# Decay rows of a fused forgetting attention: full-height selection matmuls, row DMAs and dummy matmuls in place of 3-row matmuls

## The chip, the cores and the metric

The kernel runs on one core of one Trainium2 chip. A core has five engines with an in-order instruction stream each: TensorE (PE, with its weight loads shown apart as PEld), VectorE (DVE), ScalarE (ACT), GpSimd (POOL) and SyncE (SP), which here only issues DMAs. TensorE writes to PSUM, which ScalarE and VectorE read and GpSimd does not. The metric is the device time of one launch in microseconds, lower is better.

## The reference

Attention with a forget gate, followed by a gated feed-forward with a short convolution over the sequence. B = 8 batches, H = 8 heads, S = 576 positions, D = 64, model width 512, inner width 1024.

```python
scores = np.matmul(q, k.transpose(0, 1, 3, 2)) / np.sqrt(D)
cum    = np.cumsum(np.log(np.clip(f, 0.0001, 1.0)), axis=-1)
decay  = cum[:, :, :, None] - cum[:, :, None, :]      # cum at the query minus cum at the key
scores = np.where(causal, -1e9, scores + decay)        # causal: keys after the query
attn   = exp(scores - max) / sum                       # softmax over the keys
x      = (attn @ v), heads side by side                # (B, S, 512)
h      = np.maximum(x @ w_in, 0.0)                     # (B, S, 1024)
conv   = conv_w[0] * h[s-1] + conv_w[1] * h[s] + conv_w[2] * h[s+1]
out    = (h * sigmoid(conv)) @ w_out
```

## The kernel before

The work is cut into 16 half batches (hb 0 to 15, four heads each; batch b is half batches 2b and 2b+1) and, per batch, a feed-forward of eight blocks of 128 inner columns.

**Loads.** The queue of SP loads q and k of a half batch with transposing DMAs (line 168) into one of four tiles `qk0` to `qk3`, head dimension on the partitions. The fp32 input is taken as pairs of 16-bit words, so the 64 dimensions stand on the 64 odd partitions as bf16 and the even partitions hold the low halves, which are not wanted. For the first six half batches VectorE's `clamp` (line 175) sets the even partitions to zero; later ones get them overwritten by DMAs (`fill`).

**Decay.** The decay is added inside the score matmul: even partitions 0, 2 and 4 carry 1 and -1 on one side and cum, as a bf16 high and low part, on the other. `kc` (128 x 576, bf16) holds -8 cum of all 64 heads: high parts on partitions 0 to 63, low parts on 64 to 127. VectorE makes it at the start from f by a clip (line 292), a scan (295) and two steps (296, 297), with a logarithm on ScalarE in between. From `kc` the rows reach the matmuls in four ways:

- Half batch 0: `first_rows` copies rows of `kc` by small DMAs from POOL and ScalarE (lines 236 to 239) onto partitions 0, 2 and 4 of `qk0`, first for heads 0 and 1, then for 2 and 3.
- Half batches 1 to 3 (`0 < hb < NX`): the rows stay apart. `own_rows` copies them by POOL DMAs (line 184) onto three neighbouring partitions of a feed-forward tile, `hg0`, and each score matmul (line 328) is followed by one with only these three rows (line 332), added into the same PSUM block.
- Half batches 4 and 5: `rows_of` (lines 188, 189, POOL) copies them from a DRAM image of `kc` (`decay_image`) onto the even partitions after the clamp.
- From half batch 6 on: `fill` (lines 193, 195, SP) does this for all even partitions from constants and the image.

**Score blocks.** A head's lower triangle is cut into four diagonal blocks (128 x 128, `diag_scores`), four blocks of the rest (448, 64, 320 and 192 columns, `off_scores`) and a last 64-column block (`tail_scores`): nine matmuls and 1,600 columns per head. Two heads form a pair: one diag task (8 matmuls), two off tasks (4 each); a half batch has two pairs and one tail task (4). ScalarE takes the exponential (lines 355, 365, 340), POOL masks diag and tail (368, 343). One sweep of 40 matmuls (line 390) with ones gives the sums (`sums`), two with v give the product (`pv`); VectorE forms the reciprocal (398 to 400) and normalises into `xt` (407). v is loaded per batch (line 245) and cast (251, 253) by VectorE for batch 0 and by POOL after that.

**Feed-forward.** `ffn1` (8 matmuls, line 417), relu on ScalarE (421), convolution in two VectorE steps (427, 429), tanh on ScalarE (432), gate on VectorE (436), `ffn2` (lines 443, 448), evacuation and store. w_in and w_out are loaded and cast during the first half batches (lines 216, 222, 224; 227, 231).

**Order.** `ORDER` holds one string per engine with a letter for each task, written out for the whole program. `Plan.play` walks through the five strings with estimated durations to assign buffers, and emits the instructions in the strings' order; on the chip semaphores hold each task until its inputs are there. There are four PSUM tiles `ps0` to `ps3` for all TensorE tasks. Everything ahead of the strings (loads of half batches 0 and 1, constants, `kc`, clamps and rows of half batch 0) is emitted first, in code order.

The score matmuls, with the line numbers of the profile:

```python
325    def scores(ps, col, hb, h, k0, q0, n):
326        tq, tk = stq_t[hb % RING], stk_t[hb % RING]
327        apart = 0 < hb < NX
328        nc.tensor.matmul(ps[:, col:col + n], tk[:, h * S + k0:h * S + k0 + 128], tq[:, h * S + q0:h * S + q0 + n],
329                         start=True, stop=not apart)
330        if apart:
331            o = own[32 * (hb - 1):32 * (hb - 1) + 3]
332            nc.tensor.matmul(ps[:, col:col + n], o[:, h * S + k0:h * S + k0 + 128],
333                             o[:, HS + 64 + h * S + q0:HS + 64 + h * S + q0 + n], start=False, stop=True)
```

Of the kernel before, what the change touches and what calls it, by code (L numbers as in the profile page):

```python
# [84 lines left out]
def kernel(  # L85
# [11 lines left out]
    nc = tc.nc  # L97
# [15 lines left out]
    NX, NCL = 4, 6  # L113
# [18 lines left out]
    lit = cpool.tile([128, 5], FP32, name="lit")  # L132
    lii = cpool.tile([128, 2], I32, name="lii")
# [25 lines left out]
    own = hgx_t[0].bitcast(BF16)  # L159
# [11 lines left out]

    def clamp(hb, side, c0, c1):
        t = qk_t[hb % RING].bitcast(U16)[:, 0:2 * HS].rearrange("p (a x) -> p a x", a=2)
        t = t[:, :, c0:c1] if side is None else t[:, side, c0:c1]
        nc.vector.tensor_scalar(t, t, lim[:, 0:1], 0.0 if 0 < hb < NX else lim[:, 1:2], op0=ALU.mult, op1=ALU.add)
# [5 lines left out]
    def own_rows(hb):  # L181
        c, p = hb * HH, 32 * (hb - 1)
        for j, side, first in ((1, 1, c), (2, 1, BH + c), (0, 0, c)):
            nc.gpsimd.dma_start(own[p + j:p + j + 1, (0 if side else HS + 64):(HS if side else 2 * HS + 64)], kc[first:first + HH])
# [48 lines left out]
    def first_rows(p, eng, lows):  # L233
        c, t, o = slice(2 * p, 2 * p + 2), qk_t[0], 2 * p * S
        if lows:
            eng.dma_start(t[4:5, HS + o:HS + o + 2 * S], kc[BH + 2 * p:BH + 2 * p + 2])
        else:
            eng.dma_start(t[2:3, HS + o:HS + o + 2 * S], kc[c])
            eng.dma_start(t[0:1, o:o + 2 * S], kc[c])

# [24 lines left out]
    nc.gpsimd.iota(lii[:, 0:1], pattern=[[0, 1]], base=0, channel_multiplier=1)  # L265
    nc.gpsimd.dma_start(cwrow, moe_conv_w)
# [5 lines left out]
    nc.gpsimd.memset(own.bitcast(FP32)[0:96, HS // 2 + 32:HS + 32], ones2)  # L272
    nc.gpsimd.memset(own.bitcast(FP32)[0:96, 0:HS // 2 + 32], minus2)
# [5 lines left out]
    nc.vector.tensor_copy(lit[:, 0:2], lii)  # L279
    nc.vector.tensor_scalar(lit[:, 3:4], lit[:, 0:1], 2.0, None, op0=ALU.is_equal)  # L280
    nc.vector.tensor_scalar(lit[:, 4:5], lit[:, 0:1], 4.0, None, op0=ALU.is_equal)
    nc.vector.tensor_tensor(lit[:, 3:4], lit[:, 3:4], lit[:, 4:5], op=ALU.add)
    nc.vector.tensor_scalar(lim[:, 1:2], lit[:, 3:4], float(0x3F80), None, op0=ALU.mult)
# [3 lines left out]
    for t in range(NVA):  # L287
        nc.vector.memset(va_t[t][64:128, :, NKB - 1, :], 0.0)
# [394 lines left out]
```

## Time and profile before

| | |
|---|---|
| Median of 3 runs | 298.72 us (294.78 to 300.27) |
| The profiled run | 294.69 us, span of its profile 293.0 us |
| Busy: PE, DVE, ACT, POOL | 265.8, 222.2, 203.5, 89.4 us |
| Weight loads (PEld) | 169.1 us |
| TensorE clock granted, mean over the span | 0.911 |
| DMA | 49.34 MB, mean 168 GB/s |

The profile is one execution, taken by the hardware profiler. A busy TensorE need not be a fast one: the granted clock (PEclk, 1.00 is full) stands beside it. "Idle before, releaser" says what an engine waited for. A line number with L is that of the kernel before, unless the text says otherwise; "x8" counts instructions.

### The profile page before, as it was taken

How to read it: one execution, taken by the hardware profiler on the slowest of the kernel's cores; microseconds unless marked ns; L12 is line 12 of the kernel's file. 1: busy time of each engine (PE TensorE's matmuls, PEld its weight loads, DVE VectorE, ACT ScalarE, POOL GpSimd, SP SyncE). 2: the span in 40 equal slices, each digit the busy share in tenths (PEclk: the TensorE clock that was granted, in tenths of full speed). 3: DMA queues.
4: the chain of work that ended last, by engine and by line, in shares of the span. 5: the costliest groups of instructions: out<-in, count | busy, mean ns of one | idle time of the engine just before them, and what ended most of it. 6: DMA issues, size and time to landing. Idle time of an engine off the chain costs nothing.

```text
span 293.0 us, 8211 instructions
## 1 busy us (share of the span) xinstructions
PE 265.8 (91%) x3508; PEld 169.1 (58%) x3508; DVE 222.2 (76%) x320; ACT 203.5 (69%) x272; POOL 89.4 (31%) x117
## 2 busy tenths in 40 slices
PE   1089999999999999899999998999799989999992
PEld 1054466535546766666667576766566767566541
DVE  5620239622806999988989899999989989999881
ACT  4055441643655999798888898889789979757751
POOL 6636100313240437512240454215401834000000
PEclk9995558955955999999999999999999999999999
DMA  7999997980007999999999999999999950012124
GB/s 158 202 214 295 195 180 177 241 218 0 4 0 191 177 186 207 151 202 275 201 193 233 238 175 284 194 185 191 202 252 215 238 167 10 0 74 91 73 90 161
DMA packets 126201, 49.34 MB, mean 168 GB/s; under 512 B 113807, under 2 KB 119679, under 8 KB 126166
## 3 DMA queue, kind: packets, MB, share of 16 engines
q1 hardware_dynamic: 125278, 48.00, 79.1%
q0 software_dynamic: 800, 0.68, 1.1%
q8 instruction: 27, 0.44, 0.7%
q10 hardware_dynamic: 88, 0.15, 0.1%
q14 instruction: 8, 0.07, 0.1%
HBM read 14.33 MB, written 10.03 MB: 83 GB/s over the span
## 4 chain that ended last, share of the span: by engine, by line
PE 72%; DVE 13%; DMA 5%; ACT 4%; issue 4%; POOL 1%; SPq 0%; DVEq 0%; ACTq 0%
PE ps L417 19%; PE ps L328 18%; PE ps L443 13%; PE ps L390 10%; PE ps L332 8%; DVE u L427 3%; DVE u L429 2%; DMA qk<-cz 2%; DVE xt L407 2%; PE ps L448 2%; DMA qk<-kc 2%; DVE hg L436 1%; PE ps L457 1%; DMA rb<-in_f_dram 1%; DVE rb L400 1%
## 5 line engine op out<-in xcount | busy, mean ns | idle before, releaser
L328 PE MATMUL ps<-qk 128*128 128x128 bf16 (+3 forms) x576 | 78.9, 256 | 13.6 <-DMA qk<-kc 10.1
L355 ACT ACTIVATE pp<-ps 128x1024 f16<-128x1024 f32 x64 | 64.8, 1026 | 23.5 <-PE ps L332 19.6
L417 PE MATMUL ps<-xt,w_in_f 128*128 128x288 f16 x512 | 72.5, 293 | 1.4 <-DVE xt L407 1.3
L368 POOL TENSOR_SCALAR_AFFINE_SELECT pp<-pd 128x1024 f16<-128x1024 f32 x32 | 38.0, 1195 | 95.3 <-ACT pd L365 95.3
L328 PEld LDWEIGHTS <-qk 128*128 128x128 bf16 x576 | 41.7, 100 | 39.2 <-issue 11.8
L427 DVE SCALAR_TENSOR_TENSOR u<-ht,cwt 128x576 f32<-128x576 f16 x64 | 55.3, 875 | 8.5 <-ACT ht L421 8.5
L417 PEld LDWEIGHTS <-w_in_f 128*128 128x128 f16 x512 | 50.0, 100 | 19.1 <-issue 2.4
L421 ACT ACTIVATE ht<-ps 128x576 f16<-128x576 f32 x64 | 41.4, 660 | 25.7 <-PE ps L417 23.0
L429 DVE SCALAR_TENSOR_TENSOR u<-ht,cwt,u 128x576 f32<-128x576 f16 x64 | 57.5, 906 | 0.6
L436 DVE SCALAR_TENSOR_TENSOR hg<-hg,ht 128x576 f16<-128x576 f16 x64 | 49.3, 787 | 11.3 <-ACT hg L432 11.2
L432 ACT ACTIVATE hg<-u,cw 128x576 f16<-128x576 f32 x64 | 48.9, 780 | 7.0 <-DVE u L429 6.9
L443 PE MATMUL ps<-w_out_f,hg 128*128 128x512 f16 x224 | 52.4, 379 | 0.0
L365 ACT ACTIVATE pd<-ps 128x1024 f32<-128x1024 f32 x32 | 32.7, 1028 | 15.9 <-PE ps L328 12.2
L443 PEld LDWEIGHTS <-hg 128*128 128x128 f16 x224 | 21.3, 98 | 21.7
L332 PE MATMUL ps<-hg 3*128 3x128 bf16 (+3 forms) x108 | 31.6, 293 | 0.0
L390 PE MATMUL ps<-pp,va 128*32 128x128 f16 (+3 forms) x1152 | 29.9, 258 | 1.6 <-issue 1.6
L407 DVE TENSOR_TENSOR xt<-ps,rb 128x576 f16<-128x576 f32 x32 | 23.6, 751 | 8.2 <-PE ps L390 7.7
L398 DVE STREAM_TRANSPOSE st<-ps 128x576 f32<-128x576 f32 x16 | 12.4, 776 | 22.8 <-PE ps L390 22.6
L390 PEld LDWEIGHTS <-va 128*32 128x32 f16 x1280 | 24.3, 105 | 8.6 <-issue 5.3
L343 POOL TENSOR_SCALAR_AFFINE_SELECT pt<-p 128x256 f16<-128x256 f32 x16 | 9.2, 575 | 44.8 <-ACT p L340 44.8
L468 ACT COPY ob<-ps 128x1024 f32<-128x1024 f32 (+1 forms) x23 | 18.2, 792 | 3.5 <-PE ps L457 1.5
L332 PEld LDWEIGHTS <-hg 3*128 3x128 bf16 x108 | 10.2, 95 | 14.5 <-issue 8.1
(77 smaller groups left out, 164.3 us busy)
## 6 DMA issues: line engine op xcount, KB each, us to landing
vf<-in_v_dram SPq DMA_DIRECT2D x32, 256.0 KB, 4.9
out_dram<-ob SPq DMA_DIRECT2D x16, 512.0 KB, 3.5
qk<-cz SPq DMA_DIRECT2D x10, 540.0 KB, 6.0
ob<-in_moe_w_out_dram SPq DMA_DIRECT2D x4, 512.0 KB, 6.3
vf<-in_v_dram SPq DMA_DIRECT2D x8, 128.0 KB
vf<-in_moe_w_in_dram SPq DMA_DIRECT2D x2, 512.0 KB, 5.5
hg<-in_moe_w_in_dram SPq DMA_DIRECT2D x2, 512.0 KB
out_dram<-ob SPq DMA_DIRECT2D x16, 64.0 KB
```

The lines of the kernel that those rows point to most:

```text
L328: nc.tensor.matmul(ps[:, col:col + n], tk[:, h * S + k0:h * S + k0 + 128], tq[:, h * S + q0:h * S + q0 + n], start=True, stop=not apart)
L332: nc.tensor.matmul(ps[:, col:col + n], o[:, h * S + k0:h * S + k0 + 128], o[:, HS + 64 + h * S + q0:HS + 64 + h * S + q0 + n], start=False ...
L355: nc.scalar.activation(pp_t[slot[t_dg, "p"]][:, 1024 * s:1024 * (s + 1)], ps_t[slot[t_sc, "ps"]], AF.Exp, scale=SCALE)
L368: nc.gpsimd.affine_select(pp_t[slot[t_dg, "p"]][:, 2048:3072].rearrange("p (m j) -> p m j", j=128), pd_t[slot[t_ex, "pd"]].rearrange("p (m ...
L390: nc.tensor.matmul(ps[32 * h:32 * (h + 1), AB + q0:AB + q0 + n], left_of(h, m), p, start=x in (0, 3), stop=x in (2, 9), skip_group_check=True)
L417: nc.tensor.matmul(ps[:, MB + 288 * a:MB + 288 * (a + 1)], w_in_f16[:, cc, 128 * ff:128 * (ff + 1)], xt[:, cc, 288 * a:288 * (a + 1)], sta ...
L421: nc.scalar.activation(ht_t[slot[t_m1, "ht"]][:, 1:1 + S], ps_t[slot[t_m1, "ps"]][:, MB:MB + S], AF.Relu, scale=0.5)
L427: nc.vector.scalar_tensor_tensor(u, ht[:, 0:S], cwt[:, ff, 0:1], ht[:, 1:1 + S], op0=ALU.mult, op1=ALU.add)
L429: nc.vector.scalar_tensor_tensor(u, ht[:, 2:2 + S], cwt[:, ff, 1:2], u, op0=ALU.mult, op1=ALU.add)
L432: nc.scalar.activation(hg_t[slot[t_g0, "hg"]][:, ff, :], u_t[slot[t_u, "u"]], AF.Tanh, scale=cw[:, ff, 1:2])
L436: nc.vector.scalar_tensor_tensor(hv, hv, 1.0, ht_t[slot[t_m1, "ht"]][:, 1:1 + S], op0=ALU.add, op1=ALU.mult)
L443: nc.tensor.matmul(o, hg[:, ff, 128 * c:128 * (c + 1)], w_out_f16[:, ff, :], start=(ff == 0), stop=(ff == NFF - 1))
```

## The change

Half batches 0 and 1 are now treated alike, half batches 2 and 3 like 4 and 5, and no 3-row matmul is left.

- **First pairs (heads 0 and 1) of half batches 0 and 1** (`apart`): no rows are copied. After each score matmul two full-height matmuls add the decay straight from `kc`: one with `kc` as weights and a moving operand that is one column of `sel_k` (it picks the head's high and low part) read n times, and one with `sel_q` as weights (-1 in the head's row) and `kc` as moving operand.
- **Their second pairs (heads 2 and 3)**: `own_rows` copies three rows by POOL DMAs onto partitions 0, 2 and 4 of the `qk` tile, after the clamp of that part.
- **Half batches 2 and 3**: `rows_of`, from the DRAM image, after the clamp. The tile `hg0` no longer holds rows, and its two preset memsets go.
- **Dummy matmuls** (`WARM`): 16 of 512 columns at the start on a tile of ones, and 4, 6 and 6 ahead of the first diag task of half batches 1, 2 and 3; their results are overwritten.
- The clamp of the first pair of half batch 0 moves ahead of logarithm and scan; half batch 1 is clamped in four parts instead of two. All five order strings are new.

```diff
-    NX, NCL = 4, 6
+    NCL = 6
+    WARM = {0: 16, 2: 4, 4: 6, 6: 6}
...
+    def apart(hb, h):
+        return hb < 2 and h < 2
...
-    def own_rows(hb):
-        c, p = hb * HH, 32 * (hb - 1)
-        for j, side, first in ((1, 1, c), (2, 1, BH + c), (0, 0, c)):
-            nc.gpsimd.dma_start(own[p + j:p + j + 1, ...], kc[first:first + HH])
+    def own_rows(hb, side):
+        c, t = hb * HH + 2, qk_t[hb % RING]
+        if side:
+            nc.gpsimd.dma_start(t[2:3, HS + 2 * S:HS + 4 * S], kc[c:c + 2])
+            nc.gpsimd.dma_start(t[4:5, HS + 2 * S:HS + 4 * S], kc[BH + c:BH + c + 2])
+        else:
+            nc.gpsimd.dma_start(t[0:1, 2 * S:4 * S], kc[c:c + 2])
...
+    nc.vector.memset(xt_t[0][:, 0, :], 1.0)
+    nc.vector.tensor_scalar(sel_k, hfx, lit[:, 2:3], None, op0=ALU.is_equal)
+    nc.vector.tensor_scalar(sel_q, hfx.unsqueeze(3).broadcast_to((128, 2, 2, 128)), lit[:, 0:1], -1.0,
+                            op0=ALU.is_equal, op1=ALU.mult)
+    for x in range(WARM[0]):
+        nc.tensor.matmul(ps_t[0][:, 0:512], xt_t[0][:, 0, 0:128], xt_t[0][:, 0, 64:576], start=True, stop=True)
...
     nc.vector.tensor_scalar(fsb, fsb, 1e-4, 1.0, op0=ALU.max, op1=ALU.min)
+    clamp(0, None, 0, 2 * S)
     nc.scalar.activation(fsb, fsb, AF.Ln)
...
-    for p in range(2):
-        clamp(0, None, 2 * p * S, 2 * (p + 1) * S)
-        first_rows(p, nc.gpsimd, False)
-        first_rows(p, nc.scalar, True)
-    own_rows(1)
+    clamp(0, None, 2 * S, 4 * S)
+    own_rows(0, 1)
+    own_rows(0, 0)
...
-        apart = 0 < hb < NX
-        nc.tensor.matmul(ps[:, col:col + n], tk[:, h * S + k0:h * S + k0 + 128], tq[:, h * S + q0:h * S + q0 + n],
-                         start=True, stop=not apart)
-        if apart:
-            o = own[32 * (hb - 1):32 * (hb - 1) + 3]
-            nc.tensor.matmul(ps[:, col:col + n], o[:, h * S + k0:h * S + k0 + 128],
-                             o[:, HS + 64 + h * S + q0:HS + 64 + h * S + q0 + n], start=False, stop=True)
+        o = ps[:, col:col + n]
+        nc.tensor.matmul(o, tk[:, h * S + k0:h * S + k0 + 128], tq[:, h * S + q0:h * S + q0 + n],
+                         start=True, stop=not apart(hb, h))
+        if apart(hb, h):
+            nc.tensor.matmul(o[0:m], kc[:, k0:k0 + m], sel_k[:, hb, h:h + 1].broadcast_to((128, n)),
+                             start=False, stop=False)
+            nc.tensor.matmul(o, sel_q[:, hb, h, :], kc[:, q0:q0 + n], start=False, stop=True)
...
     def diag_scores(me, i):
+        for x in range(WARM.get(i, 0) if i else 0):
+            nc.tensor.matmul(ps_t[slot[me, "ps"]][:, 0:512], kc[:, 0:128], kc[:, 64:576], start=True, stop=True)
...
-        "PE": "wdodtodooodtosopopsppffdftfoodoodffftodoofsoppsdpotpodoffffggfodtfogsodgoppofddsfoppoohoftffgfdo"
+        "PE": "wdootdodooosdtopopsppffffdodfofotfofddooostoppdosdopoptffffoggtdfdofosgdogpofpstddfpopooohffffgtd"
```

In the PE strings d is a diag task, o off, t tail, s sums, p pv, f ffn1, g ffn2, w the transposes of the convolution weights. Both programs do half batches 0 and 1, then ffn1 of batch 0 around half batches 2 and 3.

Three places where the instructions of an engine change. First TensorE where it passes from half batch 0 (tile `qk_78`, in the changed program `qk_82`) to the first diag task of half batch 1 (`qk_79`, then `qk_83`). Before:

```order
L328 LDWEIGHTS qk_78
L328 MATMUL ps_122<-qk_78 128x192
L328 LDWEIGHTS qk_79
L328 MATMUL ps_124<-qk_79 128x128
L332 LDWEIGHTS hg_117
L332 MATMUL ps_124<-hg_117 128x128
```

and changed (line 368 is a dummy, 336 the score matmul, 339 and 341 the selections):

```order
L336 LDWEIGHTS qk_82
L336 MATMUL ps_129<-qk_82 128x192
L368 LDWEIGHTS kc
L368 MATMUL ps_128<-kc 128x512
...
L336 LDWEIGHTS qk_83
L336 MATMUL ps_128<-qk_83 128x128
L339 LDWEIGHTS kc
L339 MATMUL ps_128<-sel_k,kc 128x128
L341 LDWEIGHTS sel_q
L341 MATMUL ps_128<-kc,sel_q 128x128
```

The pair of one full and one 3-row matmul per block has become three full ones, behind four dummies.

Second VectorE at the start, from the clip of f (`rb`) to the first row copies. Before:

```order
L292 TENSOR_SCALAR rb_106<-rb_106 128x576
L295 SCALAR_TENSOR_TENSOR rb_107<-one_73,rb_106 128x576
L296 TENSOR_SCALAR kc<-rb_107 128x576
L297 SCALAR_TENSOR_TENSOR kc<-rb_107,kc 64x576
L175 TENSOR_SCALAR qk_78<-qk_78,lim 128x2x1152 x2
L175 TENSOR_SCALAR qk_79<-qk_79,lim 128x2304
```

and changed:

```order
L301 TENSOR_SCALAR rb_110<-rb_110 128x576
L182 TENSOR_SCALAR qk_82<-qk_82,lim 128x2x1152
L305 SCALAR_TENSOR_TENSOR rb_111<-one_73,rb_110 128x576
L306 TENSOR_SCALAR kc<-rb_111 128x576
L307 SCALAR_TENSOR_TENSOR kc<-rb_111,kc 64x576
L182 TENSOR_SCALAR qk_82<-qk_82,lim 128x2x1152
L182 TENSOR_SCALAR qk_83<-qk_83,lim 128x1152
```

The first pair's clamp has moved ahead of the scan, and with it the scan waits for the first q and k.

Third POOL, from its first row copies on. Before:

```order
L238 DMA qk_78<-kc 1x2x576
L239 DMA qk_78<-kc 1x2x576
L238 DMA qk_78<-kc 1x2x576
L239 DMA qk_78<-kc 1x2x576
L184 DMA hg_117<-kc 1x4x576 x3
L343 AFFINE_SELECT pt_95<-p_101 128x256
L368 AFFINE_SELECT pp_88<-pd_99 128x1024
L184 DMA hg_117<-kc 1x4x576 x6
L368 AFFINE_SELECT pp_89<-pd_100 128x1024
```

and changed, from the last masks of half batch 1 on (`qk_84` and `qk_85` belong to half batches 2 and 3, `qk_82` now to 4):

```order
L378 AFFINE_SELECT pp_95<-pd_104 128x1024
L351 AFFINE_SELECT pt_100<-p_106 128x256
L198 DMA qk_84<-image 1x16x144
L199 DMA qk_84<-image 2x2304
L198 DMA qk_85<-image 1x16x144
L199 DMA qk_85<-image 2x2304
L351 AFFINE_SELECT pt_101<-p_105 128x256
L378 AFFINE_SELECT pp_96<-pd_103 128x1024
L378 AFFINE_SELECT pp_97<-pd_104 128x1024
L198 DMA qk_82<-image 1x16x144
L199 DMA qk_82<-image 2x2304
```

The rows of half batches 2 and 3, copied ahead of time from `kc` before, now pass POOL between masks and wait there for their clamps.

93 lines of the change are left out of this document (46 added, 47 removed), and 8 rows, old and new, of the table KINDS.

## The prediction

> **What bounds the kernel now.** I read the page's head first, then a table of stretches cut where the granted clock changes, then one source line in short windows, then waits, chain and transfers.
>
> ```profile
> span 293.0 us, 8211 instructions
> ...
> PEclk9995558955955999999999999999999999999999
> ```
>
> The clock row, 40 slices of 7.3 us, reads 5 tenths in seven of the first thirteen: a TensorE that is busy there is slow. The stretches (length, then busy time and instruction count of PE, PEld, DVE, ACT, POOL; clock; DMA share; GB/s):
>
> ```profile
> 15.90:22.40 6.50, 6.50 (x49) 4.59 (x49) 1.69 (x3) 4.54 (x6) 3.01 (x5) 1.00 1.15 227
> 22.40:46.30 23.90, 23.90 (x301) 12.53 (x298) 6.88 (x13) 9.70 (x11) 5.56 (x8) 0.50 1.16 218
> 46.30:60.00 13.70, 12.99 (x94) 7.56 (x83) 11.40 (x15) 7.07 (x10) 3.82 (x5) 1.00 0.93 220
> 60.00:73.60 13.60, 13.60 (x55) 6.11 (x55) 2.55 (x4) 4.71 (x6) 2.71 (x3) 0.50 0.33 86
> 73.60:80.50 6.90, 6.90 (x44) 3.94 (x42) 5.76 (x8) 4.29 (x7) 1.93 (x5) 0.99 0.03 4
> 80.50:94.10 13.60, 13.60 (x167) 7.03 (x170) 3.98 (x7) 7.58 (x9) 3.31 (x4) 0.50 0.33 84
> 94.10:286.20 192.10, 186.06 (x2806) 125.82 (x2794) 179.65 (x239) 161.32 (x222) 59.49 (x65) 1.00 0.84 173
> ```
>
> Two kernels stand here. From 94.1 the clock is full and both TensorE (186.06 of 192.10) and VectorE (179.65) are packed; I leave that stretch as it is. Before it lie 15.9 us of start and a front of 78.2 us, 51.1 of them at half clock with TensorE never idle and VectorE nearly so (2.55 of 13.60). Next, the 3-row matmuls of line 332 alone, in windows that each end at or next to a decision (busy time, count, clock, DMA share, GB/s), and their group on the page:
>
> ```profile
> 42.90:46.30 3.40, 0.00 (x0) 0.50 0.87 143
> 49.70:53.10 3.40, 1.69 (x9) 1.00 0.54 122
> 56.60:60.00 3.40, 2.33 (x10) 1.00 1.21 233
> 70.20:73.60 3.40, 0.00 (x0) 0.50 0.00 0
> 77.00:80.40 3.40, 2.29 (x11) 1.00 0.04 7
> ...
> L332 PE MATMUL ps<-hg 3*128 3x128 bf16 (+3 forms) x108 | 31.6, 293 | 0.0
> ```
>
> The clock fell after 56.6 to 60.0 and 77.0 to 80.4, where these fill over two thirds of the time, held after 49.7 to 53.1, where they fill half, and rose after the two windows with none. The changes lie 23.9, 13.7, 13.6, 6.9 and 13.6 us apart: 7, 4, 4, 2 and 4 times 3.41, so it is decided once per 3.41 us. The 2806 matmuls after 94.1 hold none of line 332, and the clock never falls. I conclude that a matmul that loads 3 of 128 rows hardly counts as work to whatever sets the clock.
>
> [...]
>
> **The change, part by part.** *Start.* The first scores wait for row DMAs:
>
> ```profile
> 2.96 1.59 SPq L168 DMA_TRANSPOSE qk<-in_q_dram  x1
> ...
> 6.01 1.55 SPq L168 DMA_TRANSPOSE qk<-in_q_dram  x1
> 6.19 1.36 DVE L295 TENSOR_TENSOR_SCAN rb<-one,rb 128x576 f32<-128x576 f32 x1 [0.75 <-ACT rb L293]
> 7.58 0.46 DVE L296 TENSOR_SCALAR kc<-rb 128x576 bf16<-128x576 f32 x1
> 8.08 0.76 DVE L297 SCALAR_TENSOR_TENSOR kc<-rb,kc 64x576 bf16<-64x576 f32 x1
> ...
> 10.12 0.88 DVE L175 TENSOR_SCALAR qk<-qk,lim 128x2304 uint16<-128x2304 uint16 x1 [0.38 <-DMA qk<-in_q_dram]
> ...
> 15.90 3.58 PE L328 MATMUL ps<-qk 128*128 128x128 bf16 x29 [10.06 <-DMA qk<-kc]
> ```
>
> The second q load, issued at 6.01, landed at 10.1, 4.1 later; the first, issued at 2.96, then lands at 7.0. The clamp that now stands ahead of the scan waits for it: 7.0 to 7.9; scan to 9.3, the two kc steps to 10.5, 1.7 later than today. But the first pair then needs no row DMA: scores at 10.5 instead of 15.9, a gain of 5.4. The new constants on VectorE (a memset, four small operations) fall where it waits for f and then for this load.
>
> The 29 first matmuls are 4,480 columns in 3.5 us, 1,280 columns per us: half of what follows below, so the clock was half there, whatever the 1.00 of that row. The 16 dummies (8,192 columns) then take at most 6.4 us, from about 1.6 to 8.0, in TensorE's empty time. They cost nothing and cover at least one whole window, so the clock is full by 8. From 8.0 to 10.5 it may drop again: then 3.4 us of selection work run at half, at most 1.7 us lost, ahead of a wait that hides it.
>
> *Matmuls.* Full-clock prices, from the chain after 94 and from a timeline in the stretch to 60.0:
>
> ```profile
> 142.06 0.98 PE ps L417 x8
> 143.15 0.81 PE ps L390 x40
> ...
> 145.05 0.88 PE ps L328 x12
> ...
> 58.42 0.23 PE L328 MATMUL ps<-qk 128*128 128x128 bf16 x1
> 58.58 0.23 PE L332 MATMUL ps<-hg 3*128 3x128 bf16 x1
> ```
>
> Eight ffn1 matmuls of 288 columns in 0.98 us give 2,350 columns per us. Selections: 4 heads, 9 blocks, 2 each, 72 matmuls of 12,800 columns, 5.4 us. No row has a moving operand that is one column read again and again; between ffn1's rate and that of the 3-row alternation (a start every 0.16 us per 128 columns, 800 per us) it is 5.4 to 16; a gain is excluded, since it is added work. I take 5.4: ffn1 has full-height weights too. Dummies inside the loop: 16 of 512 columns, 3.5 us, less where they fall into a wait. Gone: 31.6 us of line 332.
>
> *Second pair of half batch 0.* Its rows are now three DMAs on POOL after the second clamp (10.5 to 11.4).
>
> ```profile
> 10.05 1.05 POOL L238 DMA_DIRECT2D qk<-kc  x1 [3.78 <-DVE qk L175]
> 11.09 0.52 POOL L239 DMA_DIRECT2D qk<-kc  x1
> ...
> qk<-kc POOLq DMA_DIRECT2D x4, 2.2 KB, 4.7
> ...
> 41.09 1.02 ACT L355 ACTIVATE pp<-ps 128x1024 f16<-128x1024 f32 x1 [3.02 <-PE ps L332]
> ```
>
> First issue 1.05, the next 0.52 each: the third at 13.0, landed 4.7 later, 17.7. TensorE and, behind the tail, ScalarE stand until then (the new ScalarE order takes the tail third). From 17.9 twelve exponentials remain for half batches 0 and 1: ten of 1.03 and two of 0.38, 11.1 us, to 29.0. Today the last ends at 42.1, and ffn1 of batch 0 starts at 46.4; now it starts at 33.
>
> *The rest of the front.* By 94.1 today's TensorE has done half batches 0 to 3 without the last two pv, and eight ffn1. At full clock 12 score matmuls (eight of a diag, four of an off) take 0.88, and a half batch has two of these, two more off (0.88) and a tail (0.12, an estimate by columns), and three sweeps of 0.81: 5.2. Four less 1.6, plus 8 x 0.98, make 27. Four sums say when the new kernel can stand there:
>
> ```profile
> 44.92 6.11 SPq L245 DMA_DIRECT2D vf<-in_v_dram  x5
> ...
> vf<-in_v_dram SPq DMA_DIRECT2D x32, 256.0 KB, 4.9
> ...
> L355 ACT ACTIVATE pp<-ps 128x1024 f16<-128x1024 f32 x64 | 64.8, 1026 | 23.5 <-PE ps L332 19.6
> ...
> L427 DVE SCALAR_TENSOR_TENSOR u<-ht,cwt 128x576 f32<-128x576 f16 x64 | 55.3, 875 | 8.5 <-ACT ht L421 8.5
> ...
> L421 ACT ACTIVATE ht<-ps 128x576 f16<-128x576 f32 x64 | 41.4, 660 | 25.7 <-PE ps L417 23.0
> ...
> L436 DVE SCALAR_TENSOR_TENSOR hg<-hg,ht 128x576 f16<-128x576 f16 x64 | 49.3, 787 | 11.3 <-ACT hg L432 11.2
> L432 ACT ACTIVATE hg<-u,cw 128x576 f16<-128x576 f32 x64 | 48.9, 780 | 7.0 <-DVE u L429 6.9
> ```
>
> TensorE: 10.5 + 27 + 5.4 + 3.5 = 46.4. Loads: v of batch 1 is issued until 51.0, and the last of its five parts (issued near 50) lands near 55; the DMA share of 1.16 from 22.4 says that the queue is full to there, and the same transfers stand ahead of it in the new order, so it gains nothing; two casts on POOL (1.5 each, an estimate by the 1,280 elements beside a mask's 1.2 for 1,024) follow, and the sweeps that need them: 58 to 60. ScalarE: 24 exponentials of 1.03 and four of 0.38, 26.2; eight relu and eight tanh, 11.5; two casts of an exponential's size, 2.1; from 13, with 3 of waiting: 56. VectorE, from 33: eight times 2 x 0.875 + 0.787, 20.3, and some 9 (an estimate: three clamps at twice the 0.88 above, two reciprocals of about 1.8, a cast): 62 at most, since today's has not done all of it by 94.1. I take **60**, 34 earlier: the loads' and VectorE's sum, which end last.
>
> *Rows of half batches 2 and 3* now go clamp, POOL, DRAM image and back, as those of 4 and 5 do today:
>
> ```profile
> qk<-image POOLq DMA_DIRECT2D x2, 9.0 KB, 3.5
> ```
>
> A clamp of at most twice 0.88, two issues of 0.5 and 3.5 make about 6: for half batch 2, whose clamp follows batch 0's last norm at 33, ready at 39. TensorE has four ffn1 and four or six dummies until 38, so it waits 0 to 2, inside the 60. Without that cover it would be 6 for each of the two.
>
> *Loads after it.* Today SP stands still, and with it the DMA shares of 0.33, 0.03 and 0.33 above:
>
> ```profile
> SPq L227 <- ACT w_out_f L231: 26.0, 1, 26.0
> ```
>
> The fourth w_out load needs a buffer that a ScalarE cast frees, ScalarE waits for slow scores, and q, k and v queue behind. Full DMA ends near 60.0 + 0.33 x 13.6 = 64.5, and the queue goes on 26 later, near 90. With ScalarE on time the wait goes, and what follows comes after that one load, from about 66: 24 earlier, against TensorE's 34. Of the missing 10, ffn2 of batch 1 (five of 1.7) can be done first, and the lead of the loads covers some; I charge 2, with 0 to 9 as bounds.
>
> **Sum.** 293.0 - 34 + 2 = 261 of span; the profiled run has 1.7 around its span (294.69): 262.7, say **263**. The median of the runs before, 298.72, stands 1.4% above that profile; the same here would be 266.
>
> **Rivals.**
> 1. *The half clock has another cause* and stays. Then 31.6 us of 3-row work go, or 22 if only the spacing counts (0.16 of each 0.23), selections and dummies cost 17.8 at half clock, the start gives 5.4: 276 to 285. For it: other work changes too where line 332 stands. Against: the five windows above and the 192 us without a fall. 0.08. [...]
> 2. *The loads keep the end.* ScalarE again reaches the w_out cast late and SP stands 20 us or more; the loads then hardly move, and of 34 only ffn2's 8.7 and a lead of some 7 remain: 279. For it: the 26.0 above. Against: the wait comes from ScalarE waiting for slow scores. 0.09.
> 3. *Slower: POOL's in-order queue.* The row DMAs of half batches 2 to 5 wait for VectorE's clamps and stand ahead of masks; both pd buffers fill, ScalarE stops, no relu reaches VectorE, the clamp comes later still. Run one after another, each half batch costs clamp and rows 6, exponentials 6.6 and sums to norm some 6 (three sweeps and VectorE's part), 18.6 for 5.2 of TensorE: 13.4 lost, four times: 317. It decides against the change once each of the four row waits exceeds 9. Against: ScalarE and VectorE are over half idle in today's front. 0.02.
>
> **How the numbers follow.** Forecast 0.76, 263, with 252 to 274 its own range (the front done at 51 to 64, loads 0 to 9). Better than 251: 0.03, TensorE's sum of 46 with little in its way. Another 0.02 lies near no change. I give 251 to 279, which reaches into the first two rivals. About 2%, 6 us, is what a measurement here can tell from no change; every case but the third and the rest lies below 292.7: faster 0.95, same 0.03, slower 0.02.
>
> **What would show it.** Clock row without fives after slice 2; no line of 3-row matmuls; first scores near 10.5 and a TensorE pause until 17.7; first ffn1 near 33; v of batch 1 landing near 55; no 26 us wait on SP; a stretch of some 192 us at the end as packed as today's. I am wrong if the clock falls while full-height selections run, if SP's wait stays, or if VectorE has gaps after 60.

## The result and the profile after

The changed kernel takes 269.28 us (median of 4 runs, 267.36 to 272.60) against 297.25 us for the kernel before on the same chip (294.78 to 300.27): a ratio of 0.906, with a 95% interval of 0.893 to 0.919. The forecast was 263, 6 below. The profiled run took 268.24 us with a span of 266.5, where the sum had 261.

From the page of the changed kernel: head, busy times, granted clock in 40 slices (6.7 us each), and the row of the queue that SP fills (packets, MB, share of 16 engines' span; it was 79.1% before).

```profile
span 266.5 us, 8203 instructions
...
PE 236.8 (89%) x3501; PEld 158.2 (59%) x3504; DVE 224.5 (84%) x327; ACT 202.5 (76%) x272; POOL 85.5 (32%) x113
...
PEclk9989999999999999999999898999999999999998
...
q1 hardware_dynamic: 125278, 48.00, 90.5%
```

The row of fives is gone: the mean clock rose from 0.911 to 0.978. TensorE is busy 29 us less (265.8 before), with nearly the same instructions; DVE, ACT and POOL are busy as long as before. The front is read from its windows (length, busy time and count of PE, PEld, DVE, ACT, POOL; clock; DMA share; GB/s) and from the first ffn1 matmuls (min/median/max ns, first and last start in 30 to 70 us):

```profile
12.30:15.70 3.40, 3.40 (x19) 1.94 (x17) 2.07 (x9) 0.44 (x1) 1.55 (x4) 0.50 1.17 229
15.70:32.80 17.10, 14.85 (x334) 11.04 (x337) 9.37 (x16) 12.58 (x15) 8.45 (x12) 1.00 1.16 242
32.80:66.90 34.10, 25.96 (x448) 18.94 (x442) 33.85 (x40) 28.81 (x38) 17.24 (x21) 1.00 1.18 230
...
L427 PE MATMUL ps<-xt,w_in_f x95: 282/286/296, 33.1 to 70.0; 128*128 128x288 f16 x95
```

From 15.7 to 66.9 the clock is full; in the kernel before, 51.1 of the 78.2 us from 15.9 to 94.1 were at half. PE has idle time here again (25.96 of 34.10) while VectorE has none (33.85): in this part of the front VectorE and the loads now set the pace. By the starts in the trace, the work that TensorE had done at 94.5 in the kernel before (half batches 0 to 3 without two pv, and eight ffn1) is done at 60.6, 33.9 earlier.

The rest is where the missing microseconds lie. Two stretches behind the front, first of the kernel before, then of the changed one:

```profile
94.00:172.00 78.00, 76.22 (x1169) 52.62 (x1158) 72.64 (x97) 70.14 (x96) 28.49 (x32) 1.00 1.07 205
172.00:198.00 26.00, 24.99 (x473) 17.62 (x475) 25.38 (x35) 22.27 (x32) 10.85 (x13) 1.00 1.06 214
```

```profile
60.00:138.00 78.00, 74.35 (x1141) 50.25 (x1141) 71.72 (x96) 68.81 (x93) 30.41 (x35) 1.00 1.14 214
138.00:172.00 34.00, 28.57 (x498) 19.67 (x496) 24.44 (x35) 24.07 (x33) 10.60 (x11) 0.90 1.08 201
```

The first 78 us hold about the same number of instructions in both, and so does the stretch behind it (473 and 498 matmuls, 35 and 35 on DVE), which takes 34 us where it took 26. To compare kernels with different orders I marked, in each trace, when TensorE has done 27, 100 and 125 us of full-clock work in its own order (decay matmuls and dummies not counted). The marks are estimates from full-clock prices per matmul; two traces of the changed kernel differ by 1 to 2 us in them (60.6 and 59.3 below), so smaller differences say nothing:

| Work of TensorE | before | changed |
|---|---|---|
| first 27 us, done at | 94.5 | 60.6 |
| 27 to 100 | 76.9 | 78.5 |
| 100 to 125 | 26.8 | 34.1 |
| 125 to the last matmul | 88.9 | 87.8 |

Inside the 34 us, four windows show two pauses and their aftermath, and the chain of waits names what the second one waits for (start, length, what):

```profile
142.00:145.40 3.40, 0.85 (x18) 0.88 (x19) 2.52 (x3) 0.64 (x3) 0.45 (x1) 1.00 1.20 160
145.40:148.80 3.40, 3.40 (x54) 2.13 (x52) 0.51 (x1) 2.82 (x3) 2.35 (x4) 0.51 0.90 180
155.70:159.10 3.40, 1.05 (x46) 0.85 (x46) 3.04 (x6) 1.37 (x3) 0.00 (x0) 1.00 1.05 123
159.10:162.50 3.40, 3.40 (x36) 2.27 (x37) 1.41 (x2) 1.86 (x3) 1.22 (x2) 0.50 1.16 241
```

```profile
by line: DMA qk<-cz 23.8%; DMA qk<-in_q_dram 21.2%; PE ps L427 18.9%; PE ps L336 12.2%; SPq L172 9.8%; PE ps L400 8.8%; SPq L489 4.0%; issue 1.4%; SPq L203 0.1%
...
141.48 2.83 SPq L172
...
145.65 6.14 DMA qk<-in_q_dram
...
151.85 6.91 DMA qk<-cz
...
158.96 1.13 PE ps L336 x12
```

The chain runs through SP's queue: a k load, which is issued over 2.83 us once TensorE is through with line 427 at 141.48, then two stores, then the q load of half batch 11 with 6.14 us until it lands and its fill with 6.91, and only then scores. The first pause is a fill as well, that of half batch 10. The profile names VectorE's line 439 for this wait, but the weight load of the scores also waits for the fill's two DMAs, issued at 136.98 and 137.98, and they are complete only at 144.33, 0.2 us before the scores start. The DMA share in the windows is 0.90 to 1.20: the queue is full, and late. Each pause costs twice, since the clock is half in the window after it (0.51 and 0.50 with PE busy all through). The two waits were 3.08 and 2.35 us long, and in the windows ahead of the half clock PE was busy for 0.85 and 1.05 us of 3.40.

### The profile page after: what moved, and what is told of

It reads as the page before. It is cut to its first block, busy times and chain, and to the rows that moved or that the text cites. A ratio compares the mean times of both kernels' runs of the same rounds, so it can differ in the third digit from the quotient of the medians.

```text
span 266.5 us, 8203 instructions
## 1 busy us (share of the span) xinstructions
PE 236.8 (89%) x3501; PEld 158.2 (59%) x3504; DVE 224.5 (84%) x327; ACT 202.5 (76%) x272; POOL 85.5 (32%) x113
## 4 chain that ended last, share of the span: by engine, by line
PE 56%; DMA 13%; DVE 12%; SPq 7%; ACT 5%; issue 5%; DVEq 0%; ACTq 0%
PE ps L453 16%; PE ps L427 15%; PE ps L336 10%; PE ps L400 8%; DMA qk<-in_q_dram 6%; DMA qk<-cz 5%; SPq L172 4%; PE ps L467 3%; DVE u L437 2%; ACT pp L363 2%; DVE u L439 2%; DVE qk L182 2%; ACT pd L375 2%; DMA qk<-image 2%; PE ps L458 1%
## 5 line engine op out<-in xcount | busy, mean ns | idle before, releaser
L336 PE MATMUL ps<-qk 128*128 128x128 bf16 (+3 forms) x576 | 62.5, 244 | 15.7 <-DVE u L439 5.5
L427 PE MATMUL ps<-xt,w_in_f 128*128 128x288 f16 x512 | 71.6, 290 | 0.7 <-DVE xt L417 0.4
L378 POOL TENSOR_SCALAR_AFFINE_SELECT pp<-pd 128x1024 f16<-128x1024 f32 x32 | 40.3, 1264 | 77.5 <-ACT pd L375 77.4
L336 PEld LDWEIGHTS <-qk 128*128 128x128 bf16 x576 | 38.1, 99 | 31.6 <-issue 12.9
L439 DVE SCALAR_TENSOR_TENSOR u<-ht,cwt,u 128x576 f32<-128x576 f16 x64 | 55.5, 879 | 0.6
L446 DVE SCALAR_TENSOR_TENSOR hg<-hg,ht 128x576 f16<-128x576 f16 x64 | 51.8, 818 | 3.4 <-ACT hg L442 3.2
L400 PE MATMUL ps<-pp,va 128*32 128x128 f16 (+3 forms) x1152 | 26.7, 239 | 2.3 <-issue 1.9
L400 PEld LDWEIGHTS <-va 128*32 128x32 f16 x1280 | 21.8, 97 | 10.4 <-issue 8.3
L253 POOL CAST va<-vf 128x1024 f16<-128x1024 f32 x14 | 16.6, 1188 | 17.7 <-DMA vf<-in_v_dram 17.6
L400 PE MATMUL ps<-pp,ones_h 128*32 128x128 f16 (+3 forms) x576 | 14.4, 245 | 1.3 <-DVE xt L417 0.7
```

What stands on the lines that cost most here:

```text
L336: nc.tensor.matmul(o, tk[:, h * S + k0:h * S + k0 + 128], tq[:, h * S + q0:h * S + q0 + n], start=True, stop=not apart(hb, h))
L378: nc.gpsimd.affine_select(pp_t[slot[t_dg, "p"]][:, 2048:3072].rearrange("p (m j) -> p m j", j=128), pd_t[slot[t_ex, "pd"]].rearrange("p (m ...
L400: nc.tensor.matmul(ps[32 * h:32 * (h + 1), AB + q0:AB + q0 + n], left_of(h, m), p, start=x in (0, 3), stop=x in (2, 9), skip_group_check=True)
L427: nc.tensor.matmul(ps[:, MB + 288 * a:MB + 288 * (a + 1)], w_in_f16[:, cc, 128 * ff:128 * (ff + 1)], xt[:, cc, 288 * a:288 * (a + 1)], sta ...
L439: nc.vector.scalar_tensor_tensor(u, ht[:, 2:2 + S], cwt[:, ff, 1:2], u, op0=ALU.mult, op1=ALU.add)
L446: nc.vector.scalar_tensor_tensor(hv, hv, 1.0, ht_t[slot[t_m1, "ht"]][:, 1:1 + S], op0=ALU.add, op1=ALU.mult)
```

## The experiments

The theory: the whole gain is TensorE's clock, which the alternation with 3-row matmuls pulled down. Rivals: the new orders, the row DMAs or the dummies bring part of it; the clock fell for another reason; or the alternation costs time of its own, whatever the clock. Then, for the missing 6 us: the loads, or an engine's order. "before" in the ratios is the kernel before on the same chip (medians 295.97 and 295.79).

| Run | us | ratio to before, 95% interval | first 27 us done at | from there to the last matmul |
|---|---|---|---|---|
| before (profile shown) | | | 94.5 | 192.6 |
| changed (profile shown) | 269.28 | 0.906 (0.893 to 0.919) | 60.6 | 200.4 |
| e1 full rows | 267.04 | 0.899 (0.891 to 0.908) | 63.2 | 194.1 |
| e2 32 rows | 295.26 | 0.997 (0.991 to 1.002) | 92.4 | 193.5 |
| e3 no rows (one run) | 261.12 | | 60.2 | 193.4 |
| e4 3-row selection | 281.11 | 0.950 (0.944 to 0.956) | 75.4 | 198.5 |
| e5 changed kernel again | 269.70 | 0.912 (0.903 to 0.921) | 59.3 | 202.1 |
| e6 no dummies | 269.90 | 0.910 (0.901 to 0.919) | 62.2 | 201.9 |
| e7 less v | 257.76 | 0.869 (0.859 to 0.878) | 59.0 | 190.6 |
| e8 rows by DMA | 274.64 | 0.928 (0.921 to 0.935) | 74.0 | 193.3 |
| e9 64 rows | 294.96 | 0.998 (0.993 to 1.002) | 102.4 | 190.6 |
| e10 96 rows | 267.32 | 0.902 (0.895 to 0.909) | 60.5 | 196.2 |
| e11 selections only | 271.02 | 0.914 (0.910 to 0.918) | 66.9 | 195.9 |
| e12 clamp for half batch 9 | 267.95 | 0.903 (0.897 to 0.909) | 61.8 | 197.7 |

The last two columns are of the profiled run; that of e9 took 300.52 us, 5.6 more than its median, so its front is late by about as much. e1 to e3 and e8 to e11 stand on the kernel before and keep its orders, e8 but for a few places; e4 to e7 and e12 stand on the changed one.

### One part alone: the height of the extra matmul (e1, e2, e9, e10)

All four are the kernel before in its own order, with the operands of line 332 changed and little else. In e1, e9 and e10 the extra matmul adds a negligible term (a factor of 2^-20), so the decay of half batches 1 to 3 is left out. In e1 it is one matmul of all 128 partitions (line 334 there):

```diff
+    nc.gpsimd.memset(tiny, 2.0 ** -20)
...
-            o = own[32 * (hb - 1):32 * (hb - 1) + 3]
-            nc.tensor.matmul(ps[:, col:col + n], o[:, h * S + k0:h * S + k0 + 128],
-                             o[:, HS + 64 + h * S + q0:HS + 64 + h * S + q0 + n], start=False, stop=True)
+            kk = min(k0, S - 128)
+            nc.tensor.matmul(ps[:, col:col + n], kc[:, kk:kk + 128], tiny[:, 0:n], start=False, stop=True)
```

> The kernel before, with each 3-row matmul replaced by one full-height matmul of as many columns (weights from kc, a constant of 2^-20 as moving operand), so the decay of half batches 1 to 3 is left out; order, loads, waits and row DMAs stay. Theory A (3-row matmuls count as no work and lower the clock): no half clock after 22, ffn1 of batch 0 near 36 instead of 46, the later stretch of 192 us unchanged: 268 to 277 us. Theory B (the half clock has another cause, and the gain of the change comes from its orders, its start and its loads): clock falls as before, 290 to 297 us.

e2 keeps the rows where they are and reads 32 partitions instead of 3:

```diff
-            o = own[32 * (hb - 1):32 * (hb - 1) + 3]
+            o = own[32 * (hb - 1):32 * (hb - 1) + 32]
```

> The kernel before, with line 332 reading 32 rows instead of 3 (29 of them constants, a shift that the softmax cancels). If the clock goes by rows in use (A1), 32 of 128 is a quarter, and the clock should fall less often than before: 275 to 290 us. [...]

e9 and e10 are e1 with `kc[0:64]` and `tiny[0:64]`, and with `[0:96]`.

> The run with one full-height matmul in place of each 3-row matmul, with partitions 0 to 63 only (the decay itself stays left out, as there). Theory H (what counts is how many rows a matmul fills, by its share): half the rows count half, the windows of line 333 stay above the level at which the clock fell before, and the time is that of the full-height run, 265 to 272. Theory P (any matmul with fewer than 128 rows counts as none, as the 32-row run allowed): half clock as before, 290 to 297. In between, 275 to 288, if the clock falls in some windows only.

> The same with partitions 0 to 95. Theory H: 265 to 272, no fall of the clock in the front beyond that of the full-height run. Theory P: 290 to 297, as with 3 and with 32 rows.

The groups of the extra matmul on the pages of e1, e2 and e9, in this order (busy us, mean ns; e10 has 17.8 and 246, as e1):

```profile
L334 PE MATMUL ps<-tiny,kc 128*128 128x128 bf16 (+3 forms) x108 | 17.5, 246 | 0.0
```

```profile
L332 PE MATMUL ps<-hg 32*128 32x128 bf16 (+3 forms) x108 | 31.5, 292 | 0.0
```

```profile
L334 PE MATMUL ps<-tiny,kc 64*128 64x128 bf16 (+3 forms) x108 | 34.2, 317 | 0.0
```

Over these five heights it is a step, not a slope: 3, 32 and 64 rows give 294.96 to 297 us, 96 and 128 rows 267. 32 rows gain nothing (295.26), where A1 had 275 to 290, and neither expectation for 64 and 96 rows holds as it stands: 64 are as bad as 3 (294.96), against theory H, and 96 as good as 128 (267.32 and 267.04), against theory P. Two windows of seven us, each of all matmuls and then of the extra ones alone, show the clock beside it; first 64 rows, then 96:

```profile
62.00:69.00 7.00, 7.00 (x28) 2.80 (x27) 2.06 (x3) 2.34 (x4) 0.72 (x1) 0.50 0.10 22
...
62.00:69.00 7.00, 4.38 (x14) 1.33 (x13) 0.50 0.10 22
```

```profile
41.00:48.00 7.00, 7.00 (x79) 5.65 (x78) 7.00 (x8) 5.99 (x9) 3.94 (x5) 1.00 1.24 250
...
41.00:48.00 7.00, 5.05 (x32) 2.82 (x31) 1.00 1.24 250
```

PE counts as busy throughout in both. With 64 rows it does 28 matmuls in 7 us at half clock, with 96 rows 79 at full. The timeline shows what else differs; at full clock, 64 rows, then 96:

```profile
82.08 0.20 PE L330 MATMUL ps<-qk 128*128 128x64 bf16 x1
82.21 0.20 PE L334 MATMUL ps<-tiny,kc 64*128 64x64 bf16 x1
...
84.32 0.23 PE L330 MATMUL ps<-qk 128*128 128x128 bf16 x1
84.48 0.23 PE L334 MATMUL ps<-tiny,kc 64*128 64x128 bf16 x1
```

```profile
42.32 0.22 PE L330 MATMUL ps<-qk 128*128 128x128 bf16 x1
42.38 0.22 PE L334 MATMUL ps<-tiny,kc 96*128 96x128 bf16 x1
```

Starts lie 0.16 us apart for 128 columns and 0.13 for 64 when heights of 128 and 64 alternate, and 0.06 for 128 when they are 128 and 96. At half clock the alternation costs as much; from the kernel before, where 128 columns without it took about 0.10 at half clock (the 29 first matmuls, 4,480 columns, in 3.58 us):

```profile
60.24 0.28 PE L332 MATMUL ps<-hg 3*128 3x128 bf16 x1
60.45 0.29 PE L328 MATMUL ps<-qk 128*128 128x128 bf16 x1
```

And it is the change of height that costs, not the short matmul: in e4 (below), at full clock, two 3-row matmuls in a row start 0.07 apart, and the next full one 0.14 later.

```profile
10.42 0.23 PE L339 MATMUL ps<-sel_k,kc 3*128 3x128 bf16 x1
10.49 0.21 PE L341 MATMUL ps<-kc,sel_q 3*128 3x128 bf16 x1
10.63 0.23 PE L336 MATMUL ps<-qk 128*128 128x128 bf16 x1
```

So each change between full height and 64 or 3 rows costs about 0.1 us in these timelines: at full clock 0.16 in place of 0.06 for 128 columns, 0.13 in place of 0.03 for 64 and 0.30 in place of 0.19 for 448 (e9 against e10), at half clock 0.21 in place of about 0.10 for 128. The profile calls PE busy all through, though 128 columns without a change take about a third of that time (0.06 of 0.16).

This is a price apart from the clock, and the prediction's account of what bounds the kernel leaves it out. The 108 short matmuls of the kernel before make 216 changes, some 22 us of TensorE's time in the front (an estimate from these starts), beside the 51.1 us at half clock. Every run here that touches the short matmuls takes away both or keeps both: from 64 to 96 rows the spacing and the clock go over together (0.16 us and 0.50 in the lines above, then 0.06 and 1.00). So shown is that the alternation costs some 28 us; how much of that is the spacing and how much the clock is not. Nor is it shown what in the alternation pulls the clock down: a run of 64-row matmuls alone was not made.

The e1 edit alone gives the whole gain: 267.04, without selections, dummies, new row DMAs or new orders. Taking the matmul out altogether (no decay in half batches 1 to 3) gives only 6 us more in one run, 261.12, 4 below what was expected:

```diff
-            nc.tensor.matmul(ps[:, col:col + n], o[:, h * S + k0:h * S + k0 + 128],
-                             o[:, HS + 64 + h * S + q0:HS + 64 + h * S + q0 + n], start=False, stop=True)
+            pass
```

> The kernel before without line 332; the decay of half batches 1 to 3 is left out. Theory A: the clock stays full from 19 on, and the time is that of the full-height run or 1 to 4 us less, since 108 full-height matmuls are only 8 us of TensorE in a front that ScalarE, VectorE and loads pace: 265 to 275. Theory B: only the work of line 332 goes; half clock stays where it was: 275 to 285.

Its front is done at 60.2, no earlier than in the changed kernel (60.6) or with 96 rows (60.5): the 108 matmuls of 96 rows are nearly free there. The earlier start counts for as little: the first scores of e3 and e10 come at 14.0 and 14.8, against 11.1 in the changed kernel, and their fronts end when its own does.

### One part undone: short selections in the changed kernel (e4)

```diff
-            nc.tensor.matmul(o[0:m], kc[:, k0:k0 + m], sel_k[:, hb, h:h + 1].broadcast_to((128, n)),
+            nc.tensor.matmul(o[0:m], kc[0:3, k0:k0 + m], sel_k[0:3, hb, h:h + 1].broadcast_to((3, n)),
...
-            nc.tensor.matmul(o, sel_q[:, hb, h, :], kc[:, q0:q0 + n], start=False, stop=True)
+            nc.tensor.matmul(o, sel_q[0:3, hb, h, :], kc[0:3, q0:q0 + n], start=False, stop=True)
```

> The changed kernel, with both selection matmuls of the first pairs reading 3 rows instead of 128, same columns (the decay of these heads is left out). Theory A: the clock falls between 15 and 27 us, TensorE's selections go at half clock with starts 0.16 to 0.21 us apart, ffn1 of batch 0 starts 3 to 8 us after 33: 272 to 279 us. Theory B: no change of clock, 267 to 272 us.

281.11 us, and this window, where the changed kernel has 1.00 from 15.7 on:

```profile
13.00:43.00 30.00, 29.78 (x203) 12.68 (x203) 8.39 (x19) 11.60 (x13) 9.91 (x14) 0.50 1.19 238
```

With everything else of the change in place, the 72 short matmuls of half batches 0 and 1 alone bring 30 us of half clock back, and 11 us of time, 2 more than the expectation's upper end.

### The dummies, and the orders (e5, e6, e11, e8)

e5 is the changed kernel once more, beside e6 without any dummy:

```diff
-    WARM = {0: 16, 2: 4, 4: 6, 6: 6}
+    WARM = {0: 0}
```

> The changed kernel as it is, beside the runs of this call: 267 to 272 us, the same as its first runs.

> The changed kernel without any dummy matmul. Theory A (the gain is the 3-row matmuls; the clock fell after the dummies anyway, and the front is paced by ScalarE, VectorE and loads): first scores at half clock until about 15 to 18, ffn1 of batch 0 at 33 to 35, within 2 us of the changed kernel. Theory C (dummies hold the clock through the gaps between 33 and 50): half clock in one to three windows there, 3 to 10 us slower than the changed kernel.

269.70 and 269.90: no difference that these runs can tell. Without dummies the clock does fall, to 0.50 behind a stretch in which PE is busy for 4.19 of 7.60 us:

```profile
33.00:40.60 7.60, 4.19 (x34) 2.98 (x32) 7.04 (x10) 4.87 (x7) 1.04 (x2) 1.00 1.11 207
40.60:47.40 6.80, 4.96 (x31) 3.66 (x32) 5.42 (x7) 3.94 (x5) 0.64 (x2) 0.50 1.10 211
```

But PE still has idle time at half clock (4.96 of 6.80): it isn't what the front waits for, so the fall costs little, 62.2 instead of 59.3 for the first 27 us of work, and nothing at the end.

e11 takes the old orders and puts the changed kernel's two selection matmuls after every score matmul of half batches 1 to 3, with no row DMAs for them:

```diff
-            o = own[32 * (hb - 1):32 * (hb - 1) + 3]
...
+            o = ps[:, col:col + n]
+            nc.tensor.matmul(o[0:m], kc[:, k0:k0 + m], sel_k[:, hb - 1, h:h + 1].broadcast_to((128, n)),
+                             start=False, stop=False)
+            nc.tensor.matmul(o, sel_q[:, hb - 1, h, :], kc[:, q0:q0 + n], start=False, stop=True)
```

> The kernel before in its own order, without dummies, with the two full-height selection matmuls of the changed kernel for all heads of half batches 1 to 3 in place of the 3-row matmul and its row DMAs; the whole reference is computed. Theory A (the gain is the full-height matmul alone): 216 more matmuls of 128 rows are some 14 us of TensorE in the front against 7 in the one-matmul run (267.0), of which the loads behind give back most: 266 to 274. Rival (the new orders and row DMAs carry part of the gain): 276 to 285.

```profile
L340 PE MATMUL ps<-sel_k,kc 128*128 128x128 bf16 (+3 forms) x108 | 25.0, 249 | 0.0
L342 PE MATMUL ps<-kc,hg 128*128 128x128 bf16 (+3 forms) x108 | 23.4, 247 | 0.0
...
34.00:65.00 31.00, 28.88 (x396) 22.11 (x392) 23.16 (x30) 20.19 (x28) 11.91 (x15) 1.00 1.02 204
```

271.02 us, with an interval of the ratio that lies within that of the changed kernel. Its front is done at 66.9, 3.7 and 6.4 later than with the one extra matmul of e1 and e10 and 6.3 later than the changed kernel's, and what follows is 4.5 shorter than there (195.9). The new orders, row DMAs and dummies together add nothing at the end that these runs can tell.

e8 goes the other way: the old orders but for a few places, with the rows of half batches 1 to 3 by POOL DMAs into the `qk` tile behind the clamp, and no extra matmul of any kind.

```diff
+        nc.gpsimd.dma_start(t[2:3, HS:2 * HS], kc[c:c + HH])
+        nc.gpsimd.dma_start(t[4:5, HS:2 * HS], kc[BH + c:BH + c + HH])
+        nc.gpsimd.dma_start(t[0:1, 0:HS], kc[c:c + HH])
...
-        apart = 0 < hb < NX
+        apart = False
```

> The kernel before, with the rows of half batches 1 to 3 copied from kc onto the qk tile after its clamp (three POOL DMAs each), so neither 3-row nor selection matmuls, no dummies, and the old orders but for a few places (first rows and one diag task later). Full decay. Theory A: all of the gain without the extra TensorE work: between the run without line 332 and the changed kernel, 260 to 269 us. Theory B' (new orders and the earlier start are needed for the gain): over 272 us.

```profile
PE ps L326 <- DMA qk<-kc: 24.1, 5, 8.1
```

274.64, above the 272 from which the expectation would have had the new orders needed; but e11 keeps the old ones and has the gain. In e8 TensorE has no extra matmul, as in e3, and waits 24.1 us for rows (five waits, the longest 8.1), where e3 waits 9.0 us in two. Behind such waits the clock falls as well: its mean is 0.76 from 33 to 60 and 0.85 from 60 to 74. The first 27 us of work are done at 74.0, against 63.2 in e1. This is what the selections buy: scores that need no row DMA.

### The missing 6 us (e7, e3, e12)

e7 loads, from batch 3 on, only the last 64 positions of v:

```diff
-        for kb in range(NKB):
+        for kb in (range(NKB) if b < 3 else (NKB - 1,)):
```

> The changed kernel with only the last 64 positions of v loaded from batch 3 on (stale v used, output wrong for these batches): about 5 MB of 49 less, the queue of SP shorter by some 4 us per batch. If loads cause the slow stretch from 139 to 173 us (D1), TensorE is not idle there, the clock does not fall, and the time is 5 to 9 us under the changed kernel. If it is VectorE or the order of TensorE's own tasks (D2), the pause stays: within 2 us of the changed kernel.

```profile
138.00:172.00 34.00, 34.00 (x601) 23.74 (x597) 32.53 (x46) 31.85 (x45) 12.70 (x14) 1.00 0.95 185
```

257.76, 12 us less, where 5 to 9 were expected, with the same instructions on the engines. The 34 us from 138 hold 601 matmuls in place of 498, and work 100 to 125 takes 25.0 in place of 34.1. The pauses belong to the loads. Whether fewer loads would help the old orders as much was not tried.

But the last column of the table says that late loads are not enough. e3 has its front done at 60.2, moves the same 48.00 MB through SP's queue, and keeps the old orders; its part behind the front takes 193.4. Of its trace the stretch from 138, and SP's issues of v of batch 2 and of the fill of half batch 10; then the same issues in the changed kernel; and that of v of batch 2 in the kernel before:

```profile
138.00:172.00 34.00, 32.98 (x576) 22.86 (x568) 33.28 (x44) 30.14 (x41) 14.18 (x16) 1.00 1.00 205
...
61.15 6.20 SPq L245 DMA_DIRECT2D vf<-in_v_dram  x5
...
127.08 0.95 SPq L193 DMA_DIRECT2D qk<-cz  x1
```

```profile
62.02 6.77 SPq L247 DMA_DIRECT2D vf<-in_v_dram  x5
...
136.98 0.95 SPq L203 DMA_DIRECT2D qk<-cz  x1
```

```profile
89.04 5.56 SPq L245 DMA_DIRECT2D vf<-in_v_dram  x5
```

In e3 and the changed kernel the queue starts that part within 1 us, and by half batch 10 the new order's fill is 10 us later, though TensorE has done its first 100 us of work at the same time (139.3 and 139.1). In every run with the old orders the part behind the front takes 191 to 196, in every one with the new orders and the whole of v 198 to 202. So the pause comes with the new order, which brings the fills of half batches 9 to 11 late, and goes when a part of the loads goes. In SP's strings one step fits this: the new one puts the v load of batch 4 ahead of the fill of half batch 9, and that of batch 5 ahead of half batch 10's, where the old one has each load behind its fill; they hold SP for 4.31 and 5.87 us in the changed kernel. No run moved them alone, and TensorE's own string differs too, so which of the five strings it is was not separated.

e12 tries one step of that order: half batch 9 is cleared by VectorE's clamp and gets its rows by POOL DMAs, so that one fill less stands in SP's queue.

```diff
-        elif hb < NCL:
+        elif hb < NCL or hb == 9:
```

> The changed kernel with half batch 9 cleared by VectorE's clamp (1.8 us) and its rows by two POOL DMAs, in place of the fill on SP's queue (0.6 MB, some 3.5 us of the queue at 122). If the load queue sets the pace from 125 to 175, work 100 to 125 takes 30 to 32 us instead of 34 and the time is 266 to 268 against 269.7. If VectorE's order is what holds there, the same time or 2 us more.

```profile
130.00:140.00 10.00, 6.74 (x81) 3.81 (x82) 6.20 (x10) 6.68 (x9) 3.12 (x5) 1.00 1.21 218
...
117.70 7.90 DMA qk<-in_q_dram
...
128.00 5.21 DMA qk<-image
...
133.26 1.17 PE ps L336 x16
```

267.95 against 269.70, with overlapping intervals: no proof of a gain. Work 100 to 125 falls to 25.3, further than the 30 to 32 expected, but 75 to 100 rises from 26.3 to 29.4: half batch 9's q load takes 7.90 us, clamp and rows come behind it, and TensorE now stands still until 133. Moving one fill moved the pause. Of the kernels that leave nothing out of the computation, e12 has the lowest median, but none beats the changed kernel by more than these runs can tell.

## Why the prediction was right, and where it was off

**What bounds the kernel.** Right in what had to go, and only half right in why. One edit to the height of line 332 (e1) moves the time from 296 to 267, and shortening the selections (e4) brings half clock back (0.50 from 13 to 43). The conclusion drawn on the way, that a 3-row matmul "hardly counts as work", was too narrow: 64 rows behave like 3 (294.96 us, half clock). And the account blames the clock alone, while the alternation also spaces the starts, 0.16 us in place of 0.06 at full clock, some 22 us in the front by the estimate above. The forecast of the front did not suffer, because its sum of 27 prices every remaining matmul at full clock and without alternation, and so takes out both costs, named or not.

**Start.** Scores were to begin at 10.5; the first block's decay could be added at 11.1:

```profile
1.96 5.36 PE L295 MATMUL ps<-xt 128*128 128x512 f16 x16 [1.96 <-DVE xt L281]
...
11.11 0.23 PE L339 MATMUL ps<-sel_k,kc 128*128 128x128 bf16 x1 [2.32 <-DVE kc L307]
...
7.68 0.82 DVE L182 TENSOR_SCALAR qk<-qk,lim 128x2304 uint16<-128x2304 uint16 x1 [2.67 <-DMA qk<-in_q_dram]
```

The q load that the clamp waits for landed at 7.68, not 7.0. The dummies ended at 7.3, and the clock did fall from 12.3 to 15.7 (0.50), in the window behind a wait, as the prediction allowed, though its last line counts a fall under full-height selections as a sign of being wrong. The wait that was to hide this did not come: the second pair's rows landed at 16.4, not 17.7, and TensorE was still busy with the first pair then. ScalarE took its last exponential until 28.9, and ffn1 of batch 0 started at 33.1, where 29.0 and 33 stood. The earlier start has little part in it: with the old start e10 and e3 reach ffn1 at 33.9 and 34.5.

**Matmuls.** Selections run at ffn1's rate, as chosen from a range of 5.4 to 16: from 11.11 on, 23 matmuls of 128 columns start within 1.24 us, 0.056 apart, some 2,300 columns per us. In e10 they are 0.06 apart as well, and this is the price that the alternation raises to 0.16, with 64 rows (e9) and with 3 (before).

**The rest of the front.** 60 forecast, 60.6 measured, and by the terms that were to end last: VectorE is busy 33.85 of 34.10 us to 66.9, and the last cast of batch 1's v ends at 60.1. The rows of half batch 2 were to be ready at 39 with a wait of 0 to 2; they landed at 41.1, and TensorE waited 2.42 us until 41.19.

**Loads after it.** This is the step that failed: the charge of 2 for loads that come late, on a stretch left "as it is". The parts that it rests on held. SP's 26 us wait for the w_out cast is gone, and v of batch 2 is issued at 62.02, 27 earlier than in the kernel before, where 24 stood, against TensorE's 34. With the old order in the part behind, these late loads cost 0.8 in e3, 1.5 in e1, 3.3 in e11 and 3.6 in e10 (against 192.6), so 2 was about right for that order. But the new strings run to the end of the program, and the prediction took that part as packed as today's without looking at what SP's new string does there. Gaps of VectorE after 60 were named as a sign of being wrong, and they came: it is busy 24.44 of the 34.00 us from 138. Measured: 200.4 from 60.6 to the last matmul, 7.8 more than before, where 2 was charged; 7.3 of it in work 100 to 125, where each pause also halves the clock behind it (0.51 and 0.50). The sum closes: 261, plus 0.6 for the front and 5.8 here, is 267.4, beside 266.5.

**Rivals.** A half clock with a cause other than the short matmuls is excluded by e1, e9 and e10. That the spacing counts apart from the clock, as one half of this rival has it, is not excluded, as said above. "The loads keep the end" was half true: not by the cast and not at 279, but with fewer loads the kernel is 12 us faster (e7). POOL's in-order queue would have given 317 and a late front; the front was done at 60.6. POOL did stand twice until a clamp was done, for 7.86 and 8.30 us, but no mask behind it had its input yet.

## What to carry to other kernels

Read the granted clock beside TensorE's busy time: here a matmul stream that alternated 128 rows with 3 looked busy (13.60 of 13.60 us from 60.0), lost about 0.1 us at each change of height and ran at half clock for 51.1 of 78.2 us, and full-height matmuls that do the same arithmetic with many zeros were far cheaper than the 3-row ones (e11, 271.02 us against 295.79). Where several edits go in together, try the one that the profile names alone; here the height of the matmul in one line gave all of it (e1, without that decay, and e11, with it), and the orders written for the shorter front lost some 7 us later, where a queue that was already full (DMA share 1.13 from 66.9 to 142.0) met a new sequence of loads.

## What the runs showed of the hardware

- The same 108 matmuls between full-height ones give 294.96 us with 64 of 128 rows (e9) and 267.32 with 96 (e10). No height between was run.
- A change of height between 128 rows and 64 or 3 cost about 0.1 us: at full clock 0.16 instead of 0.06 from start to start for 128 columns and 0.13 instead of 0.03 for 64, at half clock 0.21 instead of about 0.10 for 128. Two 3-row matmuls in a row start 0.07 apart (e4).
- The clock was half (0.50) both with PE busy 7.00 of 7.00 (64 rows, e9) and behind real pauses (0.85 and 1.05 us busy of 3.40 in the changed kernel). There it was full again (1.00) behind the next 3.40 us, which PE was busy all through. Busy time alone does not decide it: with PE busy 3.40 of 3.40 it rose after 145.4 to 148.8 in the changed kernel and fell after 56.6 to 60.0 in the kernel before.
- Dummy matmuls bought nothing that these runs can tell (269.70 us with, 269.90 without): without them the clock fell to 0.50 from 40.6 to 47.4, but TensorE had idle time there anyway (busy 4.96 of 6.80).
